# Retention and two float32 multilayer perceptrons on one core: activations of the pair group's first token tile get a scheduling priority

## The chip, the cores and the metric

The kernel runs on one core of one Trainium2 chip. The metric is the device time of one execution in microseconds (us), the median over several runs; lower is better.

## The reference, cut to what matters

```python
x = retention(q, k, v, lam)            # B=2, H=8, S=768, D=64 -> x is 1536 tokens x 512
h = np.maximum(x @ w_in, 0.0)          # first MLP: 512 -> 2048
x = (h * h @ w_out).astype(np.float32) # 2048 -> 512
h = x @ w_in2                          # second MLP: 512 -> 2048
g = np.maximum(0.01 * h, h)            # leaky ReLU
return (g @ w_out2).astype(np.float32) # 2048 -> 512
```

The weights arrive as 64-bit floats and are read in the kernel as pairs of 32-bit words.

## The kernel before, in words

After the retention (lines 158 to 383, not touched) come the two MLPs. The 1536 tokens lie in three tiles of 512 (t = 0, 1, 2), the 2048 hidden columns of each MLP in four stages of 512 (s = 0 to 3), so the work is a list of eight stages (l, s), l being the MLP. All matmuls have operands split into a high part and a low part in a 32-bit matmul format, and each product is three matmuls: high by high, high by low, low by high (`three`, line 445).

A stage of the second MLP (l = 1) is `first_pair` (line 469), then `second` for t = 0, `first` for t = 2, `second` for t = 1 and `second` for t = 2 (line 619). `first_pair` computes the hidden values of the tiles 0 and 1 together from seven block products for each half h of the stage's columns, with sums of weight blocks (`sw`) and of token blocks (`t2` to `t4`, `xhi1`); the partial results are added on VectorE by `plus` (line 507). `put` (line 501) then calls `activate` (line 435). For l = 1 this is two leaky ReLUs on ScalarE, one into the high part `g` + tile + `h` (line 441) and one into a float32 tile `f` (line 442), and a subtraction on VectorE that leaves the low part, `g0l` for tile 0 and `g1l` for tile 1 (line 443). `second` reads those parts as the stationary operand: for each of four 128-column blocks kk of the hidden values, in order, it loads the high part twice and then the low part, one matmul each (line 567).

Weights are converted beside this by `converting` (line 98), a generator of small steps: an absolute value on ScalarE (line 109), VectorE steps at lines 110, 111, 113, 116, 117 and 120 that build a float32 number from the two words, for the first matrix of the second MLP block sums in `weight_sums` (lines 411 to 416), then the split into high and low (lines 128 and 130). After the step of line 117 the next raw tile is fetched by a DMA on SyncE's queue. One such step is traced at each `yield` of the loops that is not `False` (lines 624 to 629); `first_pair` yields `False` from its products with S3 on, so none is traced there. Two raw tiles, two `hb` tiles and one `rb` tile are shared by successive conversions.

TensorE's order is that of the program (`manual_schedule`, line 624). The orders of VectorE, ScalarE and SyncE in the MLPs come from the framework's planner: among instructions that it takes to be ready it issues the one with the lowest priority number, and the number counts up in the order in which the instructions are traced. `tc.high_priority(offset=n)` lowers the number by n for the instructions traced inside it and restores the count at its end. The engines then run their lists strictly in that order. `plus` has an offset of 400; the activations have none.

Of the kernel before, what the change touches and what calls it, by code (L numbers as in the profile page):

```python
# [19 lines left out]
def tile_retention_then_two_mlps(  # L20
# [37 lines left out]
    def bank():  # L58
        return psum.tile([P, 512], F32, tag="ps", name="ps")

    def plain():
        return fp.tile([P, TT], F32, tag="f", name="f")
# [332 lines left out]
    g, acc, x0f, x1f, tt = {}, [None] * NTILE, {}, {}, {}  # L395

    def new_g(t, first_stage=False):
        if first_stage and t == 2:
            tags = ("sw0", "sw1")
        else:  # L400
            tags = (f"g{t % 2}h", f"g{t % 2}l")
        g[t] = [late.tile([P, KF, TT], F32R, tag=tag, name=tag) for tag in tags]
# [32 lines left out]
    def activate(l, src, r, ghi, glo):  # L435
        if l == 0:
            nc.scalar.activation(r, src, AF.Relu)  # L437
            nc.scalar.square(ghi, r)
            nc.scalar.square(r, r)  # L439
        else:  # L440
            nc.scalar.activation(ghi, src, AF.Prelu, alpha=0.01)
            nc.scalar.activation(r, src, AF.Prelu, alpha=0.01)
        nc.vector.tensor_tensor(out=glo, in0=r, in1=ghi, op=ALU.subtract)  # L443

    def three(ps, ops, start, stop, again=False):
        for n, (a, b) in enumerate(ops):
            nc.tensor.matmul(ps, a, b, start=start and n == 0, stop=stop and n == len(ops) - 1, skip_group_check=again)  # L447
# [21 lines left out]
    def first_pair(s):  # L469
        new_g(0)  # L470
        new_g(1)
        ve = nc.vector
        w = {}
        for h in range(2):
            hi, lo = wts[1, s, 0, h]
            for i in range(2):
                for j in range(2):
                    w[h, f"A{i + 1}{j + 1}"] = [x[:, 2 * j:2 * j + 2, i * P:(i + 1) * P] for x in (hi, lo)]
            for n in range(4):
                w[h, f"S{n + 1}"] = [sums[s, h][:, part, n] for part in range(2)]  # L480
        x = {
            "B11": (xhi[0][:, 0:2], xlo[0][:, 0:2]),
            "B21": (xhi[0][:, 2:4], xlo[0][:, 2:4]),
            "B22": (xhi[1][:, 2:4], xlo[1][:, 2:4]),
            "T1": (xhi[1][:, 0:2], xlo[1][:, 0:2]),
        }
        for n in (2, 3, 4):
            x[f"T{n}"] = (tt[n][:, 0], tt[n][:, 1])
        ps, s1, s2, r22 = {}, {}, {}, {}

        def product(h, where, a, b, start=True):
            if start:
                ps[h, where] = bank()
            (ah, al), (bh, bl) = w[h, a], x[b]
            ops = []
            for j in range(2):
                ops += [(ah[:, j], bh[:, j]), (ah[:, j], bl[:, j]), (al[:, j], bh[:, j])]
            three(ps[h, where], ops, start, True, not start)
            return ps[h, where]

        def put(h, src, r, i, t):
            m = 2 * h + i
            activate(1, src, r, g[t][0][:, m], g[t][1][:, m])

        def plus(h, out, where, other):
            with tc.high_priority(offset=400):
                ve.tensor_tensor(out=out, in0=ps[h, where], in1=other, op=ALU.add)

        both = range(2)
        for h in both:  # L510
            b = product(h, "A", "A11", "B11")
            s1[h] = plain()
            nc.scalar.copy(s1[h], b)
            yield True
        for h in both:
            product(h, "B", "S2", "T2")
            s2[h] = plain()
            plus(h, s2[h], "B", s1[h])
            yield True
        for h in both:  # L520
            product(h, "D", "A22", "T4")
            yield True
        for h in both:
            product(h, "C", "S1", "T1")
            yield True
        for h in both:
            product(h, "B", "S3", "T3", False)
            plus(h, s1[h], "B", s1[h])
            r22[h] = plain()
            plus(h, r22[h], "C", s1[h])  # L530
            plus(h, s1[h], "D", s1[h])
            yield False
        for h in both:
            put(h, product(h, "A", "A12", "B21", False), plain(), 0, 0)
            put(h, s1[h], s1[h], 1, 0)
            yield False
        for h in both:
            product(h, "C", "S4", "B22", False)
            plus(h, s2[h], "C", s2[h])
            yield False  # L540
        for h in both:
            put(h, r22[h], r22[h], 1, 1)
            put(h, s2[h], s2[h], 0, 1)
# [111 lines left out]
```

## Time and profile before

| | us |
|---|---|
| median of 3 runs (lowest, highest) | 585.54 (584.20, 586.94) |
| the profiled execution's own time | 584.32 |
| its span, first to last instruction | 582.5 |
| TensorE busy with matmuls | 571.4 (98%) |
| TensorE busy with weight loads | 476.1 (82%) |
| VectorE busy | 405.1 (70%) |
| ScalarE busy | 277.0 (48%) |

Busy shares are averages over the span. Weight loads overlap matmuls, and the end of a matmul is modelled, so the distance from one matmul's start to the next tells more than its duration. In the rows below PE is TensorE (PEld its weight loads), DVE is VectorE, ACT is ScalarE, SPq is SyncE's DMA queue; L443 is line 443; "A <-B" behind an idle time names what ended it.

### The profile page before, as it was taken

The page shows a single profiled execution, that of the slowest core. Times are in us where ns is not written, and L with a number is a line of the kernel's source. Part 1 is how long each engine was busy: PE and PEld are TensorE (multiplying, and loading weights), DVE is VectorE, ACT ScalarE, POOL GpSimd, SP SyncE. Part 2 cuts the span into 40 slices and gives each one's busy share as a digit, 9 for nine tenths or more (in the row PEclk, how much of TensorE's full clock was granted, in tenths as well). Part 3 has the DMA queues.
Part 4 walks back from the last instruction along what each step waited for, and adds up shares of the span by engine and source line. Part 5 has one row for each costly group of instructions (what it writes and reads, how often), then busy time and mean ns, then how long its engine had stood idle before and what let it go on. Part 6 is the DMA issues. An engine that isn't in the chain of part 4 may idle for free.

```text
span 582.5 us, 7802 instructions
## 1 busy us (share of the span) xinstructions
PE 571.4 (98%) x3099; PEld 476.1 (82%) x3099; DVE 405.1 (70%) x565; ACT 277.0 (48%) x425; POOL 46.6 (8%) x61
## 2 busy tenths in 40 slices
PE   6999999999999999999999979999999999999997
PEld 6888888888888888888888858888888888888886
DVE  3789999949248752969768999929874787316222
ACT  2344698537361661528537473633662475325110
POOL 3426000000000000000000000000203111220000
PEclk9899999999999999999999999999999999999999
DMA  8999432443104040122201215262339424562432
GB/s 175 236 206 205 159 122 95 153 136 98 47 0 132 14 145 0 61 85 73 72 1 41 82 46 191 70 214 81 45 101 237 83 60 55 69 94 55 161 110 91
DMA packets 60148, 59.75 MB, mean 103 GB/s; under 512 B 38984, under 2 KB 40272, under 8 KB 60112
## 3 DMA queue, kind: packets, MB, share of 16 engines
q1 hardware_dynamic: 56128, 52.71, 30.0%
q0 software_dynamic: 3456, 6.29, 7.9%
q8 instruction: 24, 0.39, 0.3%
q10 hardware_dynamic: 528, 0.26, 0.2%
q14 instruction: 12, 0.10, 0.1%
HBM read 46.66 MB, written 12.59 MB: 102 GB/s over the span
## 4 chain that ended last, share of the span: by engine, by line
PE 95%; DMA 2%; DVE 1%; issue 1%; SPq 0%; ACT 0%; POOL 0%; ACTq 0%; POOLq 0%
PE ps L447 88%; PE ps L268 2%; PE ps L285 2%; PE ps L336 2%; DMA raw<-in_moe_w_in 1%; PE ps L334 1%; PE ps L309 1%; DMA q<-in_q 1%; SPq L65 0%; DVE g0l L443 0%; ACT qT L272 0%; POOL kd L303 0%; DVE hb L120 0%; DVE rb L117 0%; PE ps L259 0%
## 5 line engine op out<-in xcount | busy, mean ns | idle before, releaser
L447 PE MATMUL ps<-xhi,w1h 128*128 128x512 f32 x288 | 112.1, 389 | 0.0
L447 PE MATMUL ps<-xlo,w1h 128*128 128x512 f32 x288 | 112.0, 389 | 0.0
L447 PE MATMUL ps<-xhi,w1l 128*128 128x512 f32 x288 | 112.0, 389 | 0.0
L447 PEld LDWEIGHTS ps<-xhi,w1l 128*128 128x128 f32 x288 | 54.1, 188 | 11.3
L447 PEld LDWEIGHTS ps<-xhi,w1h 128*128 128x128 f32 x288 | 54.1, 188 | 11.2 <-issue 0.2
L447 PEld LDWEIGHTS ps<-xlo,w1h 128*128 128x128 f32 x288 | 54.1, 188 | 11.2
L443 DVE TENSOR_TENSOR g0l<-f,g0h 128x512 fp32r<-128x512 f32 x60 | 41.0, 688 | 26.3 <-ACT f L439 14.9
L601 POOL DMA_DIRECT2D spill<-f x24 | 21.7, 903 | 437.0 <-ACT f L591 437.0
L447 PE MATMUL ps<-w2h,g0l 128*128 128x512 f32 (+1 forms) x132 | 50.8, 385 | 3.1 <-DVE g0l L443 3.1
L130 DVE TENSOR_TENSOR w2l<-hb,w2h 128x1024 fp32r<-128x1024 f32 x16 | 19.6, 1224 | 47.4 <-ACT w2h L128 47.2
L447 PE MATMUL ps<-w2l,g0h 128*128 128x512 f32 (+1 forms) x132 | 50.5, 383 | 0.0
L447 PE MATMUL ps<-w2h,g0h 128*128 128x512 f32 (+1 forms) x132 | 50.5, 383 | 0.0
L437 ACT ACTIVATE f<-ps 128x512 f32<-128x512 f32 x48 | 28.5, 593 | 39.5 <-PE ps L447 39.5
L591 ACT COPY f<-ps 128x512 f32<-128x512 f32 x36 | 21.1, 587 | 53.4 <-PE ps L447 51.2
L109 ACT ACTIVATE hb<-raw 128x1024 f32<-128x1024 f32 x32 | 36.8, 1154 | 16.6 <-DMA raw<-in_moe_w_in 5.6
L447 PE MATMUL ps<-g0h,w2h 128*128 128x512 f32 x112 | 43.6, 389 | 0.0
L447 PE MATMUL ps<-g0l,w2h 128*128 128x512 f32 x112 | 43.6, 389 | 0.0
L447 PE MATMUL ps<-g0h,w2l 128*128 128x512 f32 x112 | 43.6, 389 | 0.0
L117 DVE SCALAR_TENSOR_TENSOR rb<-raw,rb 128x1024 f32<-128x1024 uint32 x32 | 39.1, 1222 | 0.4
L120 DVE TENSOR_TENSOR hb<-hb,rb 128x1024 f32<-128x1024 f32 x32 | 39.1, 1222 | 0.3
L113 DVE SCALAR_TENSOR_TENSOR hb<-raw,hb 128x1024 uint32<-128x1024 uint32 x32 | 39.1, 1222 | 0.3
L128 ACT CAST w2h<-hb 128x1024 fp32r<-128x1024 f32 x16 | 16.9, 1054 | 39.2 <-PE ps L447 37.3
(125 smaller groups left out, 1106.4 us busy)
## 6 DMA issues: line engine op xcount, KB each, us to landing
raw<-in_moe_w_in SPq DMA_DIRECT2D x16, 1024.0 KB, 5.6
raw<-in_moe_w_out SPq DMA_DIRECT2D x16, 1024.0 KB, 4.8
spill<-f POOLq DMA_DIRECT2D x24, 256.0 KB, 4.3
k<-in_k SPq DMA_DIRECT2D x12, 256.0 KB, 4.9
q<-in_q SPq DMA_DIRECT2D x12, 256.0 KB, 5.1
v<-in_v SPq DMA_DIRECT2D x12, 256.0 KB, 4.9
spill<-f SPq DMA_DIRECT2D x12, 256.0 KB, 2.9
f<-spill SPq DMA_DIRECT2D x12, 256.0 KB, 2.8
```

Source lines behind the costliest of these rows:

```text
L109: nc.scalar.activation(hf, w_hi.bitcast(F32), AF.Abs)
L113: yield ve.scalar_tensor_tensor(out=hb, in0=w_hi, scalar=0xC0000000, in1=hb, op0=ALU.bitwise_and, op1=ALU.bitwise_or)
L117: yield ve.scalar_tensor_tensor(out=rf, in0=w_lo, scalar=2.0 ** -52, in1=rf, op0=ALU.mult, op1=ALU.mult)
L120: yield ve.tensor_tensor(out=hf, in0=hf, in1=rf, op=ALU.add)
L128: nc.scalar.copy(hi, hf)
L130: yield ve.tensor_tensor(out=lo, in0=hf, in1=hi, op=ALU.subtract)
L268: nc.tensor.transpose(ps[:, p, :], src[:, 2 * p:2 * p + 2, :].rearrange("s h d -> s (h d)"), ident)
L437: nc.scalar.activation(r, src, AF.Relu)
L443: nc.vector.tensor_tensor(out=glo, in0=r, in1=ghi, op=ALU.subtract)
L447: nc.tensor.matmul(ps, a, b, start=start and n == 0, stop=stop and n == len(ops) - 1, skip_group_check=again)
L591: nc.scalar.copy(spilled[m], ps)
L601: nc.gpsimd.dma_start(spill[t][m], spilled[m], accum_op=ALU.add)
```

## The change

`put` passes its activations through `high_priority`, with an offset of 400 for tile 0 and of 0 for tile 1. So all three instructions of `activate` are concerned: two on ScalarE and one on VectorE, for two halves and two blocks, in the four stages of the second MLP. Inside the block the count of priority numbers is restored at its end, for offset 0 too.

```diff
         def put(h, src, r, i, t):
             m = 2 * h + i
-            activate(1, src, r, g[t][0][:, m], g[t][1][:, m])
+            with tc.high_priority(offset=400 if t == 0 else 0):
+                activate(1, src, r, g[t][0][:, m], g[t][1][:, m])
```

## Rows read from the trace of the kernel before

**Rows 1.** The page, busy time of each engine.
```profile
PE 571.4 (98%) x3099; PEld 476.1 (82%) x3099; DVE 405.1 (70%) x565; ACT 277.0 (48%) x425; POOL 46.6 (8%) x61
```
**Rows 2.** Chain that ended last, 320 to 583 us: start, length, engine, line.
```profile
319.87 24.04 PE ps L447 x106
...
343.94 0.69 DVE f L507
344.63 0.60 DVE rb L116
...
345.83 1.14 DVE rb L117
...
347.56 1.14 DVE hb L120
348.70 0.61 DVE g0l L443
...
349.36 229.88 PE ps L447 x1024
```
**Rows 3.** Waits, 336 to 352 us: engine, awaited, total, times, longest.
```profile
PEld ps L447 <- DVE g0l L443: 4.4, 3, 2.0
PE ps L447 <- DVE g0l L443: 3.1, 3, 1.5
```
**Rows 4.** Timeline of PE, second matrix of stage (1, 0): start, length.
```profile
343.73 0.39 PE L447 MATMUL ps<-w2h,g0h 128*128 128x512 f32 x1
...
345.88 0.50 PE L447 MATMUL ps<-w2h,g0l 128*128 128x512 f32 x1 [1.53 <-DVE g0l L443]
...
349.36 0.50 PE L447 MATMUL ps<-w2h,g0l 128*128 128x512 f32 x1 [0.76 <-DVE g0l L443]
349.69 0.39 PE L447 MATMUL ps<-w2h,g0h 128*128 128x512 f32 x1
```
**Rows 5.** Timeline of PE, the same place in stage (1, 1).
```profile
410.72 0.39 PE L447 MATMUL ps<-w2h,g0l 128*128 128x512 f32 x1
...
412.76 0.39 PE L447 MATMUL ps<-w2h,g0l 128*128 128x512 f32 x1
```
**Rows 6.** Busy time by stretch: length, PE, PEld, DVE, ACT, POOL, PEclk, DMA, GB/s.
```profile
343.70:349.70 6.00, 2.94 (x11) 1.46 (x10) 5.76 (x8) 4.73 (x9) 0.00 (x0) 1.00 0.21 68
349.70:380.00 30.30, 30.30 (x135) 25.07 (x134) 28.20 (x39) 14.42 (x21) 0.00 (x0) 1.00 0.41 141
```
**Rows 7.** Timeline of ACT, stage (1, 0): when the activations ran.
```profile
341.04 0.61 ACT L442 ACTIVATE f<-ps 128x512 f32<-128x512 f32 x1
...
342.51 0.66 ACT L442 ACTIVATE f<-f 128x512 f32<-128x512 f32 x1
343.03 0.62 ACT L442 ACTIVATE f<-ps 128x512 f32<-128x512 f32 x1
...
344.03 1.18 ACT L442 ACTIVATE f<-f 128x512 f32<-128x512 f32 x2
```
**Rows 8.** Timeline of DVE, before the pauses of stage (1, 0).
```profile
341.27 1.22 DVE L113 SCALAR_TENSOR_TENSOR hb<-raw,hb 128x1024 uint32<-128x1024 uint32 x1
342.40 1.29 DVE L507 TENSOR_TENSOR f<-ps,f 128x512 f32<-128x512 f32 x2
```
**Rows 9.** Timeline of DVE, later in stage (1, 0) and in (1, 1).
```profile
379.91 1.22 DVE L120 TENSOR_TENSOR hb<-hb,rb 128x1024 f32<-128x1024 f32 x1
391.15 1.23 DVE L130 TENSOR_TENSOR w2l<-hb,w2h 128x1024 fp32r<-128x1024 f32 x1 [10.02 <-ACT w2h L128]
...
411.52 0.68 DVE L443 TENSOR_TENSOR g0l<-f,g0h 128x512 fp32r<-128x512 f32 x1
```
**Rows 10.** Timeline of SP's DMA queue, stage (1, 0).
```profile
347.02 0.37 SPq L65 DMA_DIRECT2D raw<-in_moe_w_out  x1
351.20 8.52 SPq L65 DMA_DIRECT2D spill<-f  x4
```
**Rows 11.** Timeline of ACT: the next reader of a raw tile.
```profile
366.35 1.14 ACT L109 ACTIVATE hb<-raw 128x1024 f32<-128x1024 f32 x1 [0.32 <-DVE w1l L130]
```

## The prediction

> **What bounds the kernel now.** I first read the busy times: TensorE has matmuls in flight for 98% of the span, VectorE works for 70% [rows 1]. So only a place where TensorE waits can give time. The chain that ended last shows where: from 319.87 us on it is TensorE alone, except for one stretch from 343.94 to 349.36, which is VectorE's; behind it come 229.88 us of TensorE without a break [rows 2]. The list of waits around that stretch names one cause: three waits for `g0l`, the low part of tile 0's activations [rows 3]. It is the boundary between `first_pair` and `second` of tile 0 in stage (1, 0). VectorE's part of the chain then shows what delays `g0l`: between the `g0l` subtractions stand the conversion steps of lines 116, 117 and 120 [rows 2]. They were traced earlier than the activations, so the planner put them first wherever both were ready.
>
> **The size of what can be gained.** At this place TensorE wants a new `g0l` with each third matmul. Undisturbed, in stage (1, 1), the nine matmul steps from the first `g0l` to the fourth take 412.76 - 410.72 = 2.04 us, 0.227 each [rows 5]. In stage (1, 0) nine steps, from the first matmul at 343.73 to the tenth at 349.69, take 5.96 us [rows 4]. The loss is 5.96 - 2.04 = 3.92 us, the 3.1 us of matmul waits [rows 3] and the slow restart behind each. The four boundaries are one per stage of the second MLP; the other three show no wait, since the unbroken piece of the chain holds them [rows 2]. So 3.92 us, 0.67%, is the most that the change can bring.
>
> The granted clock of TensorE in this stretch is 1.00, its 2.4 GHz level, before, through and behind the three pauses [rows 6]. The Trainium skill, "TensorE: Matmul & The Clock Gate", Part 1, says that the tensor engine is put back to its lower clock when it idles. By that rule matmuls behind the pauses could have run at half speed, and removing the pauses would give up to 11 x 0.227 = 2.5 us more to the matmuls of the stretch, counted from the rows; the trace does not agree here, so the sum has no such term.
>
> **The change part by part.**
>
> *VectorE, tile 0.* No instruction is added or removed. The four `g0l` subtractions now outrank the conversion steps. The cost of those steps on the chain was 0.60 + 1.14 + 1.14 = 2.88 us [rows 2], and the rest of the 3.92 is that `g0l` was served behind the additions of line 507, of which the last waited for TensorE until 343.94 [rows 2]. Now `g0l` also outranks those traced behind it (line 539), which only tile 1 needs. Can VectorE deliver in time? The weight load reads `g0l`, about one matmul step ahead, so the four have to end by about 343.96, 344.64, 345.32 and 346.00 (the third, sixth, ninth and twelfth matmul from 343.73 at 0.227, less one step). Their inputs from ScalarE are there at 341.65 (341.04 + 0.61), 343.17, 343.65, and for the fourth between 344.7 and 345.2 (one of the two at 344.03) [rows 7]. VectorE is busy with line 113 until 342.40 and then needs 0.60 us for the addition on which the fourth depends [rows 8]; four `g0l` at 0.61 [rows 2] follow. From 342.40 to 346.00 are 3.60 us, the work that must lie in them is 5 x 0.60 = 3.0. So all four can be in time, with room for one short step of 0.60; a long step of 1.14 in between costs about 0.5 us, two cost about 1.7. The planner never holds an engine back for something that comes soon, so one step in a gap is likely. I take 0.5 us as lost and a gain of 3.92 - 0.5 = 3.4. The ends are no gain (the order stays) and 3.92.
>
> *ScalarE, tile 0.* The same four activations now go ahead of those of tile 1. That brings the fourth `f` forward by at most one activation of about 0.6 us [rows 7]. It is in the room above and adds nothing.
>
> *Tile 1.* Offset 0 moves none of its instructions ahead; only numbers tie. Its `g1l` come later than before by the steps that were overtaken, but `second` of tile 1 starts only after `second` of tile 0 and `first` of tile 2, 48 matmuls each, 2 x 48 x 0.227 = 21.8 us later. Cost nothing; without that cover it would be the 2.88 us again.
>
> *The overtaken conversion steps.* They run up to 4 x 0.61 = 2.4 us later. What follows them in line: the weight sums and the splits of stage (1, 1), the fetch behind line 117, and what is queued behind that fetch. The fetch went out at 347.02 and the spill stores at 351.20 [rows 10]; some 2.4 us later it is still ahead of them, and the next instruction that takes a raw tile runs at 366.35 [rows 11]. VectorE is nearly full until 380, 28.20 of 30.30 us [rows 6], ends its backlog with the step at 379.91 and then idles 10.02 us until a second-matrix tile comes free [rows 9]. This idle time is the cover: with TensorE 3.4 us earlier it should shrink to some 6 to 7 us, and cost nothing. Cover gone, TensorE would wait for weights at the start of stage (1, 1).
>
> *The other three boundaries.* Nothing to gain. In stage (1, 1) the last `g0l` ran from 411.52 and ended at 412.20, and its matmul began at 412.76 [rows 5, 9]. That is a margin of 0.3 us to the weight load, one step ahead; the priority can only widen it. Nothing added.
>
> **Sum.** 3.4 us off 584.32 gives 580.9 for the profiled execution (span 582.5 to 579.1, with 1.8 us around it). The median of the runs is 585.54, 1.2 above the profiled one; on it the prediction is 582.1. Runs of the kernel before lie 2.7 us apart, so about 0.5%, 2.9 us, is what a measurement of this kernel tells from no change; the forecast lies only a little beyond it.
>
> **The rivals.**
>
> *Gaps are filled with conversions* (20%). The planner works with its own durations. If in its view `g0l` becomes ready late, it puts two or three conversion steps in the gaps, and the chip keeps part of the stall: at 1.14 us a step 1.1 to 2.4 us stay lost, the gain is 1.5 to 2.8, the time 582.7 to 584.0. For it speaks that line 113 was let in at 341.27, ahead of an addition that has the 400 [rows 8]; against it, that the inputs of the first three `g0l` are there before 343.7 [rows 7].
>
> *The order does not change* (12%). If the planner takes all four `g0l` to be ready only behind lines 116 to 120, the priority decides nothing: 585.5. Against it speaks that on the chip VectorE served line 116 when the first input had been waiting since 341.65 [rows 2, 7].
>
> *The stall moves and multiplies* (6%). VectorE is at its limit where the change acts [rows 6]. If conversions deferred here arrive late at the boundaries of stages (1, 1) and (1, 2), each could have three steps in its way as (1, 0) had, 3.92 us each: 2 x 3.92 - 3.92 = 3.9 us slower, 589.5. It decides only when the backlog exceeds the 10.02 us of idle time [rows 9], and 2.4 plus 3.9 us is less. Besides, no conversion step is traced from the S3 products on, so only such a backlog could stand there.
>
> The forecast has the remaining 62%: a gain of 3.0 to 3.9 us, 581.6 to 582.5.
>
> **How the numbers follow.** The likeliest case gives 582.1. Its own range, with a spread of the median of about 1 us, is 580.5 to 583.5. To hold 8 in 10 the range takes in the partly filled gaps and the unchanged order: 580.0 to 586.0. Faster by over 0.5% means under 582.6: most of the forecast's 62% and a little of the first rival's, less what the spread of runs takes away, 0.55. Within 0.5%: the rest of these, and the unchanged order, 0.40. Slower: 0.05.
>
> **What would show it.** Right, if in the profile of the changed kernel the waits of TensorE for `g0l` are gone or under 1 us in sum, the four `g0l` of stage (1, 0) stand ahead of lines 116, 117 and 120 on VectorE, the chain is TensorE alone from 320 us to the end, and VectorE's idle time ahead of the first `w2l` of stage (1, 1) falls from 10.0 to 6 or 7 us. The forecast is wrong if a conversion step still lies between two `g0l` with TensorE waiting, if a wait for `w1l`, `sw` or `w2l` appears at a later boundary, or if the pauses go and the time does not.

## The result and the profile after

The changed kernel takes 580.83 us in the median (580.50 to 581.29, 6 runs), the kernel before 585.96 (584.20 to 587.41, 6 runs, the three known before among them). The ratio is 0.9914 with a 95% interval of 0.9894 to 0.9934: faster by 5.1 us, between 3.9 and 6.2. The forecast was 582.1, with a range of 580.0 to 586.0. The profiled execution took 580.95 us with a span of 579.2.

The page's busy times, and the chain that ended last from 320 us on (start, length, engine, line), after:

```profile
PE 569.3 (98%) x3099; PEld 475.3 (82%) x3099; DVE 405.8 (70%) x565; ACT 276.8 (48%) x425; POOL 45.9 (8%) x61
```
```profile
319.81 256.07 PE ps L447 x1141
575.88 0.02 issue
575.90 0.42 DVE f L595
```

VectorE's stretch in the middle of the chain [rows 2] is gone: TensorE alone sets the end from 320 us on, in one piece. Line numbers behind the edit are one higher, so line 508 is `plus`. The timeline of TensorE (start, length) where [rows 4] had its pauses:

```profile
344.35 0.39 PE L447 MATMUL ps<-w2h,g0h 128*128 128x512 f32 x1
344.58 0.39 PE L447 MATMUL ps<-w2l,g0h 128*128 128x512 f32 x1
344.81 0.39 PE L447 MATMUL ps<-w2h,g0l 128*128 128x512 f32 x1
...
345.49 0.39 PE L447 MATMUL ps<-w2h,g0l 128*128 128x512 f32 x1
...
346.17 0.39 PE L447 MATMUL ps<-w2h,g0l 128*128 128x512 f32 x1
346.39 0.39 PE L447 MATMUL ps<-w2h,g0h 128*128 128x512 f32 x1
```

From the first to the tenth matmul it is now 346.39 - 344.35 = 2.04 us against 5.96, and no wait for `g0l` is listed. So the pauses are gone to the last hundredth: 3.92 us. VectorE, beside it, after:

```profile
342.28 0.69 DVE L443 TENSOR_TENSOR g0l<-f,g0h 128x512 fp32r<-128x512 f32 x1 [0.30 <-ACT f L442]
342.88 1.28 DVE L508 TENSOR_TENSOR f<-ps,f 128x512 f32<-128x512 f32 x2
344.08 0.68 DVE L443 TENSOR_TENSOR g0l<-f,g0h 128x512 fp32r<-128x512 f32 x1
344.68 0.68 DVE L508 TENSOR_TENSOR f<-ps,f 128x512 f32<-128x512 f32 x1
345.28 1.28 DVE L443 TENSOR_TENSOR g0l<-f,g0h 128x512 fp32r<-128x512 f32 x2
346.48 1.22 DVE L113 SCALAR_TENSOR_TENSOR hb<-raw,hb 128x1024 uint32<-128x1024 uint32 x1
347.62 0.69 DVE L443 TENSOR_TENSOR g1l<-f,g1h 128x512 fp32r<-128x512 f32 x1
348.22 0.69 DVE L116 TENSOR_SCALAR rb<-hb 128x1024 uint32<-128x1024 uint32 x1
```

All four `g0l` stand ahead of lines 116, 117 and 120, and of line 113 too, which had run at 341.27 before the additions [rows 8]. What was overtaken did no harm. Later in the stage, VectorE and SyncE's queue, after:

```profile
378.52 1.22 DVE L120 TENSOR_TENSOR hb<-hb,rb 128x1024 f32<-128x1024 f32 x1
387.80 1.23 DVE L130 TENSOR_TENSOR w2l<-hb,w2h 128x1024 fp32r<-128x1024 f32 x1 [8.06 <-ACT w2h L128]
```
```profile
349.43 1.52 SPq L65 DMA_DIRECT2D spill<-f  x2
351.05 0.38 SPq L65 DMA_DIRECT2D raw<-in_moe_w_out  x1
```

The idle time that covers the backlog shrank from 10.02 us to 8.06 [rows 9], and the fetch moved from 347.02 to 351.05, behind two spill stores [rows 10].

One thing does not add up yet. The two traces differ by 584.32 - 580.95 = 3.4 us, which is the 3.92 less 0.6 us by which this execution reached the place later (344.35 against 343.73). The medians differ by 5.1. And the runs of before spread over 3.2 us, those of after over 0.8.

### The profile page after: what moved, and what is told of

Its sections match the earlier page's. It is cut to its first block, busy times and chain, and to the rows that moved or that the text cites. A ratio compares the mean times of both kernels' runs of the same rounds, so it can differ in the third digit from the quotient of the medians.

```text
span 579.2 us, 7796 instructions
## 1 busy us (share of the span) xinstructions
PE 569.3 (98%) x3099; PEld 475.3 (82%) x3099; DVE 405.8 (70%) x565; ACT 276.8 (48%) x425; POOL 45.9 (8%) x61
## 4 chain that ended last, share of the span: by engine, by line
PE 95%; DMA 2%; issue 1%; POOL 0%; SPq 0%; ACT 0%; DVE 0%; POOLq 0%; ACTq 0%
PE ps L447 88%; PE ps L268 2%; PE ps L285 2%; DMA raw<-in_moe_w_in 1%; PE ps L336 1%; PE ps L334 1%; DMA q<-in_q 1%; PE ps L309 1%; PE ps L194 1%; SPq L65 0%; POOL kd L303 0%; ACT qT L272 0%; PE ps L259 0%; ACT kT L272 0%; DVE f L595 0%
```

## The experiments

Two questions stood open: which part of the change brings the gain, and what the median gains beyond the pauses in the trace. The eight experiments form two sets of four. Each set is compared with 23 runs of the kernel before (median 585.59 for the first set, 585.74 for the second). All edits are shown against the kernel before.

**The kernel before, once more.** No edit.

> The kernel before, unchanged, to see how its own runs spread and what its pauses do in another execution. Theory A (the pauses on tile 0's low parts are the whole effect): the profile shows the same three pauses, 3.9 us lost between 343 and 350 us, ratio to before 0.998 to 1.002, and the spread of runs (584.2 to 587.4) has nothing to do with the granted clock. Rival B (the pauses also cost clock in some executions, which is why the medians fell by 5.1 us and the two traces only by 3.3): runs near 587 show a mean granted clock lower by 0.002 to 0.004 than runs near 584, or the profile shows a granted clock under 1.00 between 343 and 360 us.

Measured: 585.76 us (584.00 to 587.43), ratio 1.0007 [0.9992, 1.0022]. The pauses are there again, three waits and 3.1 us of matmul waits. But the granted clock differs from that of the first trace [rows 6]. Busy times by stretch of this execution (length, PE, PEld, DVE, ACT, POOL, PEclk, DMA, GB/s), then TensorE's timeline behind the third pause:

```profile
343.70:349.70 6.00, 2.92 (x11) 1.50 (x10) 5.80 (x8) 4.68 (x9) 0.00 (x0) 1.00 0.26 68
349.70:353.70 4.00, 4.00 (x12) 3.15 (x11) 4.00 (x9) 0.59 (x1) 0.00 (x0) 0.57 0.56 225
```
```profile
349.31 0.50 PE L447 MATMUL ps<-w2h,g0l 128*128 128x512 f32 x1 [0.78 <-DVE g0l L443]
...
350.22 0.63 PE L447 MATMUL ps<-w2h,g0l 128*128 128x512 f32 x1
350.65 0.63 PE L447 MATMUL ps<-w2h,g0h 128*128 128x512 f32 x1
...
353.21 0.49 PE L447 MATMUL ps<-w2h,g0h 128*128 128x512 f32 x1
353.54 0.39 PE L447 MATMUL ps<-w2l,g0h 128*128 128x512 f32 x1
```

From 349.7 to 353.7 the granted clock is 0.57 in the mean: TensorE ran mostly at its lower level of 1.2 GHz, after a stretch in which it had stood still three times. Matmuls start 0.43 us apart instead of 0.227. The chain gives the price. Its last TensorE piece, 1024 matmuls in both executions:

```profile
349.31 231.47 PE ps L447 x1024
```

Against 229.88 [rows 2] this is 1.6 us more. The runs tell the same. The table has the 58 runs of the unchanged program in the two sets (the 12 of this experiment and twice 23), and the 30 runs of kernels without the pauses (the changed kernel and the second, fourth, sixth and eighth experiment), grouped by the mean granted clock of the run:

| mean clock | with pauses: runs, median us | without: runs, median us |
|---|---|---|
| 0.999 and over | 6, 584.3 | 7, 580.5 |
| 0.996 to 0.998 | 16, 585.5 | 17, 581.0 |
| 0.993 to 0.995 | 23, 585.6 | 6, 580.9 |
| under 0.993 | 13, 586.6 | none |

A mean clock lower by 0.003 over 582 us is 1.7 us of TensorE time, the size of one such stretch. But the mean does not say where the clock fell. In the first profile of the kernel before it fell in the retention, and so it did in the sixth experiment's profile, which has no pauses; in the control's profile it did not. The busy times by stretch of these three:

```profile
15.00:20.00 5.00, 4.89 (x53) 4.12 (x49) 3.71 (x8) 1.75 (x3) 3.06 (x4) 0.70 0.82 183
```
```profile
0.00:20.00 20.00, 15.89 (x155) 13.99 (x156) 9.72 (x35) 5.94 (x10) 7.98 (x18) 0.91 0.88 183
```
```profile
0.00:20.00 20.00, 15.21 (x159) 13.56 (x159) 11.05 (x37) 6.40 (x11) 7.91 (x18) 1.00 0.92 182
```

So the first profile (mean clock 0.996, 584.32 us) and the control's (0.997, 585.85 us) have nearly the same mean, and the one that lost its clock at the pauses is 1.5 us slower. Kernels without the pauses lose little by their falls of the clock: 0.5 us at most between the groups of the right column.

**VectorE's part alone.** `put` written out, with the priority on the subtraction only:

```diff
-            activate(1, src, r, g[t][0][:, m], g[t][1][:, m])
+            ghi, glo = g[t][0][:, m], g[t][1][:, m]
+            nc.scalar.activation(ghi, src, AF.Prelu, alpha=0.01)
+            nc.scalar.activation(r, src, AF.Prelu, alpha=0.01)
+            with tc.high_priority(offset=400 if t == 0 else 0):
+                ve.tensor_tensor(out=glo, in0=r, in1=ghi, op=ALU.subtract)
```

> Of the change only the VectorE subtraction has the priority; the two ScalarE activations of each call are traced without it. Theory A: VectorE's order at the boundary of stage (1, 0) is as in the changed kernel, no wait of TensorE for g0l, 580.8, as fast as the changed kernel within 0.3 us. Rival C (tile 0's activations going ahead on ScalarE is what brings g0l in time): a wait of 0.5 us or more stays, 582 to 585.

Measured: 580.30 us (580.11 to 581.02), ratio 0.9914 [0.9898, 0.9929]; its chain is one piece of TensorE:

```profile
319.83 255.64 PE ps L447 x1139
```

**ScalarE's part alone.** The same, with the block around the two activations instead:

```diff
-            activate(1, src, r, g[t][0][:, m], g[t][1][:, m])
+            ghi, glo = g[t][0][:, m], g[t][1][:, m]
+            with tc.high_priority(offset=400 if t == 0 else 0):
+                nc.scalar.activation(ghi, src, AF.Prelu, alpha=0.01)
+                nc.scalar.activation(r, src, AF.Prelu, alpha=0.01)
+            ve.tensor_tensor(out=glo, in0=r, in1=ghi, op=ALU.subtract)
```

> The other half: only the two ScalarE activations have the priority, the VectorE subtraction has not. Theory A: lines 116, 117 and 120 still stand between the g0l subtractions, three waits of 3.9 us in sum stay, time as before (585 to 586.5). Rival C: half or all of the gain, 581 to 583.5.

Measured: 585.68 us (583.93 to 587.89), ratio 1.0001 [0.9984, 1.0017]. In its chain the conversion steps stand where they stood (here the subtraction is line 507 and `plus` line 511):

```profile
344.28 0.60 DVE rb L116
344.88 0.60 DVE g0l L507
345.48 1.14 DVE rb L117
346.62 0.60 DVE g0l L507
347.22 1.14 DVE hb L120
348.35 0.61 DVE g0l L507
```

So the gain is VectorE's order; ScalarE's has no part in it that can be measured.

**Tile 0 alone.** Tile 1 is called without a block:

```diff
-            activate(1, src, r, g[t][0][:, m], g[t][1][:, m])
+            if t == 0:
+                with tc.high_priority(offset=400):
+                    activate(1, src, r, g[t][0][:, m], g[t][1][:, m])
+            else:
+                activate(1, src, r, g[t][0][:, m], g[t][1][:, m])
```

> The priority for tile 0 alone; tile 1 is called without the block of offset 0, so the count of priority numbers runs on there. Theory A: 580.8 as the changed kernel, the same order on VectorE. Rival D (the renumbering of tile 1 and of all that follows has a part in it): at least 0.5 us slower than the changed kernel.

Measured: 580.92 us (580.15 to 581.36), ratio 0.9921 [0.9906, 0.9937]. The offset of 0, and the renumbering that it brings, has no effect that can be measured.

**The pauses kept, but filled.** In stage (1, 0), for tile 0 and the first 128 columns, TensorE repeats matmuls that it can do already. They write to a bank that nothing reads:

```diff
-            three(ps, ops[:6], True, False)
-            yield
-            three(ps, ops[6:], False, True)
+            if (l, s, t, m) == (1, 0, 0, 0):
+                spare = bank()
+                for n, more in ((0, 6), (3, 3), (6, 3)):
+                    three(ps, ops[n:n + 2], n == 0, False)
+                    for _ in range(more):
+                        nc.tensor.matmul(spare, ops[n][0], ops[n][1], start=True, stop=True)
+                    three(ps, ops[n + 2:n + 3], False, False)
+                three(ps, ops[9:], False, True)
+                yield
+            else:
+                three(ps, ops[:6], True, False)
+                yield
+                three(ps, ops[6:], False, True)
```

> The kernel before with its pauses kept but filled: TensorE repeats 6, 3 and 3 matmuls of operands that it has already (into a bank that nothing reads) ahead of the first three uses of g0l in stage (1, 0). They take 12 x 0.227 = 2.7 us of the 3.9 in which it would stand still; the orders of VectorE and ScalarE are those of before. Theory B (pauses cost 3.9 us, and on top of it clock in part of the executions, 1.2 us in the mean): the 3.9 us stay, the clock loss goes, 584.0 to 584.8, with a spread of runs near 1 us and no mean clock under 0.994. Rival A (no clock loss, the wider spread of before has another source): as before, 585.6 with runs from 584 to 587.

Measured: 584.44 us (583.54 to 585.21), ratio 0.9977 [0.9962, 0.9993], no run under a mean clock of 0.994. TensorE's timeline (line 574 is the filling):

```profile
344.61 0.39 PE L447 MATMUL ps<-w2h,g0h 128*128 128x512 f32 x1
...
345.06 1.52 PE L574 MATMUL ps<-w2h,g0h 128*128 128x512 f32 x6
346.75 0.50 PE L447 MATMUL ps<-w2h,g0l 128*128 128x512 f32 x1 [0.17 <-DVE g0l L443]
...
350.23 0.50 PE L447 MATMUL ps<-w2h,g0l 128*128 128x512 f32 x1
350.57 0.39 PE L447 MATMUL ps<-w2h,g0h 128*128 128x512 f32 x1
```

The useful work is no faster: first to tenth matmul still takes 350.57 - 344.61 = 5.96 us. But work that nobody needs made the kernel 1.3 us faster (0.4 to 2.2 by the interval); TensorE hardly stood still any more, one matmul waited 0.17 us. That this is the clock and not another effect of the filling shows in the runs whose clock did not fall: at a mean clock of 0.999 and over, this kernel's four runs take 584.3 us in the median, and so do the six of the unchanged program in the table. So the two terms separate: 585.74 - 584.44 = 1.3 us are clock, and 584.44 - 580.9 (the next experiment) = 3.5 are the pauses, near the 3.92 of the traces.

**The steps moved in another way.** No priority; in stage (1, 0) the first eight yields of `first_pair` trace no conversion step:

```diff
-            for part in stage(l, s):
-                for room in part:
+            parts = stage(l, s)
+            for part in parts:
+                for n, room in enumerate(part):
+                    if (l, s) == (1, 0) and part is parts[0] and n < 8:
+                        continue
                     if room is not False:
                         convert()
```

> The kernel before without any priority, but in stage (1, 0) no conversion step is traced at the eight yields of first_pair ahead of its S3 products, so lines 113, 116 and 117 get numbers behind the activations. VectorE then has the four g0l ahead of them. Theory A and B alike: no wait for g0l, 580.3 to 581.2, as the changed kernel, as it is the place of the conversion steps alone that counts and not how it came about. Rival (the priority helps by another way, such as ScalarE's order or later stages): 582 or more.

Measured: 580.89 us (580.39 to 581.67), ratio 0.9916 [0.9891, 0.9941], no wait for `g0l`. What counts is where the conversion steps stand on VectorE, not by which means they were put there.

**A longer pause.** In stage (1, 0) tile 0's subtraction goes 20 numbers back:

```diff
-            activate(1, src, r, g[t][0][:, m], g[t][1][:, m])
+            ghi, glo = g[t][0][:, m], g[t][1][:, m]
+            nc.scalar.activation(ghi, src, AF.Prelu, alpha=0.01)
+            nc.scalar.activation(r, src, AF.Prelu, alpha=0.01)
+            with tc.high_priority(offset=-20 if t == 0 and s == 0 else 0):
+                ve.tensor_tensor(out=glo, in0=r, in1=ghi, op=ALU.subtract)
```

> The opposite of the change: the VectorE subtraction of tile 0 is put 20 numbers back in stage (1, 0), so three g1l (0.61 us each) and one more stand ahead of the third and fourth g0l. Theory A: TensorE's third pause grows by 1.8 us, a fourth of 0.5 us comes, nothing else: 585.6 + 2.3 = 587.9 with the spread of before. Theory B: as A, and the clock falls behind the pauses in more executions, so 0.3 to 0.7 us more, 588.2 to 588.6; a mean clock of 0.993 or less in most runs.

Measured: 588.38 us (586.79 to 589.31), ratio 1.0043 [1.0026, 1.0059]; 7 of 12 runs have a mean clock of 0.991 or less, the lowest 0.984. The size is the one that the second theory (pauses and clock) gave, but the interval, 1.5 to 3.5 us, holds that of the first (pauses alone) too. Nor does the time follow the mean clock within these runs: the two at 0.997 took 588.1 and 589.1, the profiled one, at 0.994, 586.8. So this experiment does not decide between the theories. In the profile the clock fell already during the pauses; busy times by stretch:

```profile
345.00:350.00 5.00, 2.61 (x6) 1.32 (x6) 5.00 (x8) 2.75 (x6) 0.00 (x0) 0.67 0.53 161
350.00:355.00 5.00, 4.50 (x14) 3.54 (x15) 4.96 (x10) 1.65 (x2) 0.00 (x0) 0.65 0.26 101
```

Here a part of the stretch at the lower clock lies inside the pauses, where TensorE waits anyway; whether that is why the times do not follow the clock is not shown. The expected fourth pause did not come in that execution: at the lower clock the matmul of the fourth `g0l` began at 351.94, after the end of that `g0l` at 351.6, and only its weight load had waited.

**The first stage alone.** The offset of 400 in stage (1, 0) only:

```diff
-            activate(1, src, r, g[t][0][:, m], g[t][1][:, m])
+            with tc.high_priority(offset=400 if t == 0 and s == 0 else 0):
+                activate(1, src, r, g[t][0][:, m], g[t][1][:, m])
```

> The changed kernel with the offset of 400 in stage (1, 0) alone; in the stages (1, 1) to (1, 3) it is 0. Theory: the whole gain is at the one boundary, 580.3 to 581.2 as the changed kernel. Rival (margins at the other three boundaries matter in some executions): at least 0.5 us slower than the changed kernel.

Measured: 580.86 us (580.21 to 581.73), ratio 0.9915 [0.9890, 0.9940]. The other three boundaries bring nothing, as they had no wait.

## Why the prediction was right, and where it was not

*The place and the mechanism* were right. The one stretch of the chain that was VectorE's [rows 2] is the source of the whole difference: the sixth and eighth experiment give the full gain by acting in stage (1, 0) alone, in two ways, the second gives it by VectorE's order alone, and the third gives none by leaving that order.

*The size of the pauses*, 3.92 us, was right: 5.96 became 2.04.

*The 0.5 us kept back* for a conversion step in a gap was a term mis-sized: it measured nothing. The planner put two additions and a third between the `g0l` but no conversion step, and moved line 113 away as well, which the prediction had left where it was. On the other side the last addition, which the prediction had counted as overtaken, still ran ahead of the third and fourth `g0l`. The fourth ended at 346.56 and its weight load began at 346.62, so of the 0.6 us of room that had been worked out 0.06 were left; that nothing was lost was close.

*The clock* is the step that failed. The prediction had only one execution to go by, whose granted clock is 1.00 through and behind the pauses [rows 6], and gave the term nothing. That execution, at 584.32 us, lay near the lower end of runs from 584 to 587. The prediction had set it against the rule of the Trainium skill ("TensorE: Matmul & The Clock Gate", Part 1) that an idle tensor engine is put back to its lower clock; in the control's profile, with 0.57 behind the pauses, the trace agrees with that rule. The term measures 1.6 us in that profile and 1.3 us in the median, inside the 2.5 us that the prediction had put beside its sum. With the pauses' 3.92, the clock's 1.3 and nothing kept back, the sum is 5.2 us, and 5.1 were measured.

*The number* was met with some luck. Both terms erred to the same side, so the gain was 5.1 us where 3.4 were forecast, and 580.83 lies below the 581.6 to 582.5 of the forecast's own case. It lies in the range because of the 1 us that had been allowed for the spread of the median, not because of a term that the prediction had seen.

*The median.* The prediction put the 3.4 us off the median as off the profiled execution. The 1.2 us between the two are, by the table of the runs, the clock term of other executions (584.3 against 585.5 to 585.6); the change takes them away too.

*ScalarE, tile 1 and the other boundaries* cost and brought nothing, as said. *The overtaken steps* were covered, with 8.06 us of idle time left where 6 to 7 were expected; the fetch did not stay ahead of the spill stores, which cost nothing, as the next reader of a raw tile ran at 365.50.

*The rivals* that gaps are filled, that the order stays, and that the stall moves on are excluded by the trace: no wait of TensorE is left behind 320 us.

## What to carry to other kernels

Where one engine is full, look for the stretch of the chain that is not its own, and ask of each helper's list what stands ahead of the piece that is waited for: here three background steps of 2.9 us, moved and not removed, were worth 0.9%, the clock included. A pause of TensorE can cost more than its length, and a single profile need not show it: if the runs spread by more than those of a kernel without pauses, compare the granted clock of the runs before the term is set to nothing. Filling a pause with work that nobody needs, ahead of the wait, tells the two prices apart.

## What the runs showed of the hardware

That pauses this short can lower the clock had not been expected: the longest wait for a weight load was 2.0 us, the three together 4.4 [rows 3], and matmuls ran between them. It happens in some executions and not in others: the control's profile shows the fall behind the pauses, the first profile of the same program shows 1.00 there, and so does that of the third experiment, which has the same pauses. In the runs, 13 of the 58 of the unchanged program have a mean clock under 0.993, and none of the 30 without the pauses. What decides it within one program was not settled.
